# Attention and a token-mixing MLP on one core: late weights' loads tied to ScalarE's progress, the last two blocks turned into one tile and one product, and another order table

## The chip, the cores and the metric

The kernel runs on one core of a Trainium2 chip. The metric is the device time of one execution in microseconds (us); the kernel before has a median of 632.07 us over three runs (631.93 to 632.17). In the profile PE is TensorE's matmul side and PEld its weight loads, DVE is VectorE, ACT ScalarE, POOL GpSimd, SP the sync engine that issues most DMAs.

## The reference

With S = 2048 rows, D = 512 columns, H = 32 heads of 16 columns and F = 1376 hidden units:

```python
xn = layernorm(A_x)                           # per row, no scale or bias
# A: attention
q, k, v = split_heads(xn @ A_wqkv)            # 32 heads, 16 columns each
p = softmax(q @ k^T / 4)                      # 32 x 2048 x 2048
a = join_heads(p @ v) @ A_wo
# B: an MLP over the rows (tokens)
h = layernorm(xn)
u = gelu(h^T @ B_w1 + B_b1)                   # 512 x 1376
b = (u @ B_w2 + B_b2)^T
return A_x + a + b
```

`B_x` isn't used. Inputs and output are bfloat16.

## The kernel before

**Tiles and blocks.** The 2048 query rows are cut into four parts of 512 (`qb`), the 32 heads into eight groups of four. A part and a group make a block, 32 in all (`NBLK`), which are worked through one after the other. A block's four heads are four rows `r` of it, and the 2048 keys are 16 tiles `kt` of 128, so that a block has 64 score tiles of 128 keys x 512 queries, and the whole program 2048. `score_mm` (L758) makes one with K = 32 rows of TensorE's array (a head's 16 columns, the rest of QT being zero): four such products lie on the four row quarters of the array and can run beside each other. The result goes to one of eight PSUM banks of 512 f32.

**Two ways to exponentiate.** A score tile leaves PSUM by ACT or by DVE. `exp_tile` (L773) lets ACT exponentiate one, two or three banks at once into `pT`, or into slots in the memory of `wqkv_sb` once the weights there are used up. `first_planes` (L834) lets DVE make an integer approximation of the exponential, a "plane"; `make_plane` (L843) then derives two more planes from the first, by POOL (INT64_ADD) and in one place by DVE. Planes lie in `planes` and in the memory of `x_sb`, `xn_sb`, `xnT` and `w2blk`. `pv_mm` (L777) multiplies with V: one product for a tile from ACT, three for a tile from DVE, each on one of the four column quarters of the array and all into bank 7 (`PV_BANK`), where V's extra column of ones (`V17`) adds up the softmax's denominator in row 16 of each head's 32.

**Between blocks.** When a block's 64 tiles are through, `epi_steps` (L1063) copies bank 7 to SBUF, gathers the denominators by DMA (`den_scr`), inverts them (L1089), spreads them by two more DMAs (`rec_scr`, `denb`) and multiplies (L1105) into `oT`, which the output projection `op_mm` (L1026) reads. Two neighbouring blocks share a tile of 128 rows: the odd block's heads are moved into the gaps of the even one by the DMA `OT<-OT`. Block 30 has a shortened chain of its own without that move (`last`, `nr`), and block 31 is finished at the end by `tail_epilogue` (L1276), which turns bank 7 with DVE's transposes, so that the denominator lies beside its row, inverts, multiplies and turns back into `otmp`. As 30 and 31 lie in different tiles, the last 128 rows of A_wo are applied as two products, each with half of its rows zero: `wo_pad` and `op_half` (L1031).

**The rest of the work.** The projections to Q, K and V, both layer norms, the MLP (`ut_steps`, `yo_steps`) and the output projection are cut into chains of steps that are fitted between the scores. Most products of 128 columns are issued as four of 32 (`mm_full`, L651).

**The order.** What stands where on each engine is written out by hand in the string `ORDER`, which `replay` (L1180) reads: S are scores, E an exponential on ACT, F and L planes, P a group of four products with V, C the next step of a chain, H a quarter of such a step, U a product of the tail, Z zeros, G a copy of `part` into a bank. `Sched` (L306) records the operations, works out who must wait for whom from what they read and write, and puts the waits in. Every engine then runs its own list in order, and so does SP with its DMAs: a DMA that waits holds up all behind it on SP.

**The late weights.** `late_steps` (L949) is a chain that loads what the prologue doesn't need: b1, the first two column blocks of w1 (`w1_load`), `wo_c` (all of A_wo) and the eight strips of `wo_pad`. Its steps wait for nothing but the memory that they write.

Of the kernel before, what the change touches and what calls it, by code (L numbers as in the profile page):

```python
# [9 lines left out]
BF16 = mybir.dt.bfloat16  # L10
# [5 lines left out]
D = 512  # L16
# [42 lines left out]
NW1 = 2  # L59
# [14 lines left out]
C006C00C00S3000011025E20101E152S3032103114E22334E145C00Z7C1NC011C01C01C01C01C00C01C01C01C01C01C01C01C01C1OS3045056060  # L74
C1NE25667E108C01C01C01C0j3C1TC01C0jC0jS3074085096E2459AE16BC1UC022C01C1OC02P0000P333.S30A00B10C5C1OE201CDE15EC02C034
C1VC03C03C03P66.3C046C1WC04C04C04C04C04C03C04S10D2E12FC1PS30E00F10G4E20101E142C04P9.66C0jC04C055C1PC05S20H60I2C1PE163
E126P.999C05C061C04C1XS30J40K50L0E24578E109C06C1YC1iC06C1QC06C086PCCC.C1iC08C06C1iC1QS30M40N50O2E245ABE12CC1iC071C07
C07PFF.CC07C1iC08C090C1iC1RC1iS30P40Q50R6C1QE245DEE160C09C09C09C07C07C07C07Z7C09C0A2C0AC0AC07C0AC0AC0AC0AS10S0E101C1Z
S30T40U50V1E2452FE113C07C1aC0APIIFFC1RC0B6C0BC0AC0X0C0XC0BS30W40X50Y2H0XFC1RE24567E128C0XC0AC1bC0C6C0CC0CC0CPLLIIC1c
S10Z1H0XCE119C0CC1SS30a40d50b6E3456ABCPOOLLC0E2C0jC0EC1SS10e1H0XDE11DC0jC0D3C0DC0DC0DC0DC0DC0DC0DC0ES30f40h50i6H0XEC1S  # L80
C1fE3456012PRROOC0F1C0DC0FC0FC1dC0FC0G3C0GC0GC0DC0GC0GC0GC0FC0GC0GC0Y2C0jC1eC0YC0YC0GS10c1E11EC0XS10g3E133C0YC0GC1j
S30j40k50l6E3456678C1kC0H1C0YC0HS30m20n30o0E2239FE10AC1lC0HPUURRZ7C1mZ7C1nS30p40q50r6E2450CE16BC1oPXXUUC1pC0I1C0IC1q
C0IC0IC1rC0J3C0JC0JC0JC1sC0JC0JC0JC0JPaaXXC0IC0L2C0LC0LC0JC0LC0LS20s00t1E201DEC1tS30u40v50w3E24512E133C0JC0LC1uC0LC0L
C0LC1vC0LC0LC0LC0LC1wC0LC0LC0LPddaaC1xC0Z6C0LC0ZC0ZS30x00y10z2E20167E128C1yC0LS20-40_5E2459FC1gC1gC1gC1gC1gC1gC1gC1g
C1gC1gC1gC0ZPggddC1gC0M3C0MC0ZC0MC0MC0MC0MC0MC1gC0MC0MC0MC0MC0MC0MC0MC0MC0MC0a6C0aS313014112A0H0aDE2010AC0MC0aC0M
S316417515B0H0aCE245BCF12PjjggP..jjF13S31901A118A0H0aFE20112C1-C0N3C0NC0NC0NC0NC0NC0NC0NC0NF12S21B41C5H0aEE245DEC1-C0N
# [344 lines left out]
def bass_parallel_sum__softmax_full_mha__mixer_token_mlp__prompt_kernel(  # L431
# [18 lines left out]
    with ExitStack() as es:  # L450
# [142 lines left out]
        def ld_wo():  # L593
            return dma("sp", wo_c[:, :, :], A_wo.rearrange("(T q) n -> q T n", q=128), reads=[], writes=[("wo_c",)])
# [585 lines left out]
        def replay(text):  # L1180
# [5 lines left out]
            for k in it:  # L1186
# [76 lines left out]
                elif k == "U":  # L1263
                    c, T = divmod(num(), 5)
                    if T == 4 or (T == 0 and c > 1):
                        tail_bk[c] = num()
# [101 lines left out]
```

## Time and profile before

| | |
|---|---|
| median of three runs | 632.07 us |
| the profiled execution | 631.26 us |
| its span, first to last instruction | 629.5 us |
| PE, DVE, ACT, POOL busy | 98%, 92%, 98%, 68% |
| granted TensorE clock | 1.00 of full speed throughout |
| DMA | 30.02 MB, mean 48 GB/s |

The span is from the profiled execution; the time of the same execution is 1.8 us longer than its span, and the median is 0.8 us above it. In rows of groups the columns are: line, engine, operation, what is written and read, shapes, count, then busy time in us and mean ns of one, then idle time before and who ended it. In a timeline they are start and length in us, and a bracket holds the idle time of the engine just before. Busy time counts overlapping instructions of an engine once, so a mean length can be longer than the step from one to the next.

### The profile page before, as it was taken

The page shows a single profiled execution, that of the slowest core. Times are in us where ns is not written, and L with a number is a line of the kernel's source. Part 1 is how long each engine was busy: PE and PEld are TensorE (multiplying, and loading weights), DVE is VectorE, ACT ScalarE, POOL GpSimd, SP SyncE. Part 2 cuts the span into 40 slices and gives each one's busy share as a digit, 9 for nine tenths or more (in the row PEclk, how much of TensorE's full clock was granted, in tenths as well). Part 3 has the DMA queues.
Part 4 walks back from the last instruction along what each step waited for, and adds up shares of the span by engine and source line. Part 5 has one row for each costly group of instructions (what it writes and reads, how often), then busy time and mean ns, then how long its engine had stood idle before and what let it go on. Part 6 is the DMA issues. An engine that isn't in the chain of part 4 may idle for free.

```text
span 629.5 us, 20523 instructions
## 1 busy us (share of the span) xinstructions
PE 618.9 (98%) x8776; PEld 195.6 (31%) x8776; DVE 581.6 (92%) x889; ACT 616.3 (98%) x715; POOL 429.9 (68%) x625
## 2 busy tenths in 40 slices
PE   8989999999999999999999999999999999999997
PEld 4444342222232322222223323222322222232223
DVE  7989999989989999999999999998999899989996
ACT  7989999999999999999999999999999999999995
POOL 2105666866677777767688767867887678776775
PEclk9999999999999999999999999999999999999999
DMA  8050000112202122030121031112122121223001
GB/s 235 3 119 9 17 20 5 34 36 55 56 17 53 41 49 53 21 78 7 32 48 28 20 81 37 42 45 73 43 76 51 42 72 30 62 49 74 21 20 53
DMA packets 69957, 30.02 MB, mean 48 GB/s; under 512 B 56494, under 2 KB 66734, under 8 KB 69866
## 3 DMA queue, kind: packets, MB, share of 16 engines
q1 hardware_dynamic: 69434, 28.31, 18.5%
q8 instruction: 69, 1.13, 0.7%
q10 hardware_dynamic: 432, 0.39, 0.2%
q14 instruction: 22, 0.18, 0.1%
HBM read 22.15 MB, written 2.61 MB: 39 GB/s over the span
## 4 chain that ended last, share of the span: by engine, by line
PE 71%; ACT 25%; DVE 3%; issue 0%; POOL 0%; DVEq 0%; POOLq 0%
PE ps L786 27%; PE ps L761 24%; ACT pT L774 19%; PE ps L666 18%; ACT wqkv_sb L774 6%; DVE stats L603 0%; DVE KT L691 0%; DVE x_sb L838 0%; DVE xn_sb L838 0%; DVE xn_sb L629 0%; PE ps L678 0%; DVE planes L838 0%; PE ps L1142 0%; POOL jrow L523 0%; DVE V L691 0%
## 5 line engine op out<-in xcount | busy, mean ns | idle before, releaser
L774 ACT ACTIVATE pT<-ps 128x1024 bf16<-128x1024 f32 (+2 forms) x501 | 462.2, 1026 | 2.5 <-PE ps L659 1.5
L761 PE MATMUL ps<-QT,KT 32*128 32x512 bf16 x2048 | 254.0, 384 | 1.5 <-DVE KT L691 0.3
L838 DVE TENSOR_SCALAR planes<-ps 128x512 int16<-128x512 f32 (+1 forms) x255 | 188.7, 771 | 12.2 <-PE ps L659 6.6
L774 ACT ACTIVATE wqkv_sb<-ps 128x1024 bf16<-128x1024 f32 (+1 forms) x177 | 175.1, 1028 | 0.1
L786 PE MATMUL ps<-pT,V 128*32 128x512 bf16 x954 | 156.3, 386 | 0.0
L838 DVE TENSOR_SCALAR x_sb<-ps 128x512 int16<-128x512 f32 (+1 forms) x172 | 137.5, 825 | 13.8 <-PE ps L761 8.0
L761 PEld LDWEIGHTS ps<-QT,KT 32*128 32x128 bf16 x2048 | 67.3, 90 | 239.0 <-ACT pT L774 139.6
L786 PE MATMUL ps<-planes,V 128*32 128x512 bf16 x606 | 123.2, 384 | 0.0
L786 PE MATMUL ps<-x_sb,V 128*32 128x512 bf16 x496 | 102.2, 383 | 0.0
L848 POOL INT64_ADD planes<-planes x73 | 58.7, 807 | 50.0 <-DVE planes L838 46.3
L786 PE MATMUL ps<-wqkv_sb,V 128*32 128x512 bf16 x337 | 77.3, 386 | 0.0
L848 POOL INT64_ADD x_sb<-planes x81 | 63.1, 785 | 17.0 <-DVE planes L838 9.3
L838 DVE TENSOR_SCALAR xnT<-ps 128x512 int16<-128x512 f32 (+1 forms) x91 | 70.4, 801 | 4.6 <-PE ps L761 2.1
L786 PE MATMUL ps<-planes,V17b 128*32 128x512 bf16 x297 | 73.0, 384 | 0.0
L848 POOL INT64_ADD planes<-x_sb x73 | 57.6, 795 | 21.7 <-DVE x_sb L838 15.1
L838 DVE TENSOR_SCALAR xn_sb<-ps 128x512 int16<-128x512 f32 (+1 forms) x72 | 57.9, 826 | 3.2 <-PE ps L761 1.5
L786 PE MATMUL ps<-x_sb,V17b 128*32 128x512 bf16 x217 | 54.8, 384 | 0.2 <-DVE OT L1073 0.2
L666 PE MATMUL ps<-gT,w2blk 128*32 128x512 bf16 (+1 forms) x688 | 52.9, 383 | 0.0
L666 PE MATMUL ps<-xn_sb,w1blk 128*32 128x512 bf16 x624 | 49.6, 383 | 0.0
L786 PEld LDWEIGHTS ps<-pT,V 128*32 128x32 bf16 x954 | 39.0, 94 | 33.9 <-issue 29.6
L786 PE MATMUL ps<-xnT,V 128*32 128x512 bf16 x189 | 46.3, 384 | 0.0
L666 PE MATMUL ps<-xnT,wqkv_sb 128*32 128x512 bf16 (+3 forms) x612 | 40.6, 344 | 2.9 <-issue 1.3
(122 smaller groups left out, 890.5 us busy)
## 6 DMA issues: line engine op xcount, KB each, us to landing
w1blk<-in_B_w_dram SPq DMA_DIRECT2D x10, 512.0 KB
w2blk<-in_B_w_dram SPq DMA_DIRECT2D x16, 320.0 KB
denb<-rec_scr SPq DMA_DIRECT2D x16, 256.0 KB
xres<-in_A_x_dram SPq DMA_DIRECT2D x16, 128.0 KB, 3.3
QT<-qraw SPq DMA_DIRECT2D x120, 16.0 KB, 1.8
OT<-OT SPq DMA_DIRECT2D x60, 32.0 KB, 2.0
out_dram<-osb SPq DMA_DIRECT2D x14, 128.0 KB, 1.8
x_sb<-in_A_x_dram SPq DMA_DIRECT2D x2, 512.0 KB
```

What stands on the lines that cost most here:

```text
L666: op = sc.add("pe", lambda e, sl=sl, c=c: e.matmul(dst[sl, :], lhsT=lhsT[:, sl], rhs=rhs, start=start, stop=stop, tile_position=(0, 32 * c ...
L761: return sc.add("pe", lambda e: e.matmul(bank(bk), lhsT=KT[32 * r:32 * r + 32, T, 128 * kt:128 * (kt + 1)], rhs=QT[32 * r:32 * r + 32, slo ...
L774: return sc.add("act", lambda e: e.activation(slots(us), pick(ps3, bs), ACTF.Exp, scale=EXP_SCALE), reads=[("bank", b) for b in bs], write ...
L786: return sc.add("pe", lambda e: e.matmul(bank(PV_BANK)[32 * r:32 * r + 32, :], lhsT=vt_[:, off:off + 32], rhs=rhs, start=start, stop=stop, ...
L838: return sc.add("dve", lambda e: e.tensor_scalar(pick(plane_i[pb].rearrange("p (r n) -> p r n", n=512), ss), pick(ps3, bs), BIAS + SHIFT[0 ...
L848: return sc.add("pool", lambda e: e.int64_add(plane_q[pb][:, 0:128 * n], plane_q[pb0][:, 0:128 * n], -down * LANES), reads=rd, writes=wr, ...
```

## The change

It has three parts.

**Loads.** The two first loads of w1, the load of `wo_c` and the strips of the last weights are given one more dependence: the instruction that ACT was given last when the load was recorded (`extra=sc.streams["act"][-1:]`). SP issues such a load only when ACT is through with that instruction. In the order table the load steps now stand far apart.

**The end.** Block 30 takes the way of block 31: at its end `turned` turns bank 7 with two transposes into `ot`, `turned_rec` inverts 16 denominators per row, and `turned_mul` writes the result to columns 16 to 31 of each 32 of the tile `tb` (the memory of `zer`). Block 31 writes columns 0 to 15 of it. The tile is turned back once for both into `otmp`, and one product with `wo_s`, the last 128 rows of A_wo in the order that fits (strips of 16 swapped in pairs), takes the place of the two with `wo_pad`. Of the four strips of 128 output rows at the end (c = 0 to 3), ACT finishes the odd ones and DVE the even ones, in the order 0, 1, 2, 3; before, ACT finished 0 and 1, DVE 2 and 3, in the order 0, 2, 1, 3.

**The order.** The whole table is another one. It gives 1285 score tiles to ACT and 763 to DVE, where before it was 1291 and 757. ACT's exponentials of two tiles stay 601; those of one tile go from 71 to 47, those of three from 6 to 12. DVE's first planes of one tile go from 491 to 529, those of two tiles from 133 to 117. PE has 8778 instructions in both.

```diff
 ORDER = """
-C006C00C00S3000011025E20101E152S3032103114E22334E145C00Z7C1NC011C01C01C01C01C00C01C01C01C01C01C01C01C01C1OS3045056060
+C006C00C00S3000011022E3012012C00S3033104115E3345345Z7C00C1NC016C01C01S3040051062C1NE3012678C01C1TC01C01C01C01C01C01C0
...
-            return dma("sp", wo_c[:, :, :], A_wo.rearrange("(T q) n -> q T n", q=128), reads=[], writes=[("wo_c",)])
-
-        def ld_wop(e_, r):
+            return dma("sp", wo_c[:, :, :], A_wo.rearrange("(T q) n -> q T n", q=128), reads=[], writes=[("wo_c",)],
+                       extra=sc.streams["act"][-1:])
+
+        def ld_wos(e_, r):
+
             row = 3 * 128 + 32 * r + 16 * e_
-            return dma("sp", wo_pad[32 * r:32 * r + 16, e_, :], A_wo[row:row + 16, :], reads=[],
-                       writes=[("wo_pad", e_, r)])
+            p0 = 32 * r + 16 * (1 - e_)
+            return dma("sp", wo_s[p0:p0 + 16, :], A_wo[row:row + 16, :], reads=[], writes=[("wo_s", e_, r)],
+                       extra=sc.streams["act"][-1:])
...
-            z += [lambda bk, ft=ft: w1_load(ft) for ft in range(NW1)]
-            return z + [lambda bk: ld_wo()] + [lambda bk, e_=e_, r=r: ld_wop(e_, r) for e_ in range(2) for r in range(4)]
+            z += [lambda bk, ft=ft: w1_load(ft, sc.streams["act"][-1:]) for ft in range(NW1)]
+            return z + [lambda bk: ld_wo()] + [lambda bk, e_=e_, r=r: ld_wos(e_, r) for e_ in range(2) for r in range(4)]
...
-        def op_half(par, e_, sti, bk, first, last):
-            src = oT[:, par, 3, 128 * sti:128 * (sti + 1)] if e_ == 0 else otmp[:, 128 * sti:128 * (sti + 1)]
...
+        def op_last(sti, bk):
+            return mm_full(bank(bk), otmp[:, 128 * sti:128 * (sti + 1)], wo_s[:, :], 128, 512, False, True,
+                           [("otmp", sti)] + [("wo_s", e_, r) for e_ in range(2) for r in range(4)], bk)
...
+        def turned(dst, keys):
+
+            for h in range(2):
+                sc.add("dve", lambda e, h=h: e.transpose(dst[:, hs[h]], bank(PV_BANK)[:, hs[h]]),
+                       reads=[("bank", PV_BANK)], writes=[keys[h]])
+
+        def turned_rec(src3, c, rk, key, dk):
+            sc.add("dve", lambda e: e.reciprocal(den128[:, dk, c], src3[:, c, 16]), reads=[key], writes=[rk])
+
+        def turned_mul(src3, c, rk, key, dk, i0, zk):
+            n = c.stop - c.start
+            sc.add("dve", lambda e: e.tensor_tensor(tb3[:, c, i0:i0 + 16], src3[:, c, 0:16],
+                                                    den128[:, dk, c].unsqueeze(2).broadcast_to([128, n, 16]), ALU.mult),
+                   [key, rk], zk)
...
+            if b == NBLK - 2:
+
+                ot3 = ot.rearrange("p (c i) -> p c i", i=32)
+                c = slice(0, 16)
+                return [lambda bk: turned(ot, [ok, ok]), lambda bk: turned_rec(ot3, c, ("den", pi), ok, pi),
+                        lambda bk: turned_mul(ot3, c, ("den", pi), ok, pi, 16, [("zer",), ("zer2",)])]
...
-                dst, key = (osb[:, c, :], ("osb", c)) if c < 2 else (xres[:, c - 2, :], ("xres", c - 2))
-                if c < 2:
+                dst, key = (osb[:, c // 2, :], ("osb", c // 2)) if c % 2 else (xres[:, c // 2, :], ("xres", c // 2))
+                if c % 2:
                     copy("act", dst, bank(bk), [("bank", bk)], [key])
...
-            for c in (0, 2, 1, 3):
+            for c in range(4):
                 fin(c)
```

What moves on SP, early in the program: `QT<-qraw` spreads a block's queries, `den_scr`, `OT<-OT`, `den`, `rec_scr` and `denb` are the steps between blocks, `w1blk`, `wo_c` and `wo_pad` or `wo_s` the late loads. Before:

```order
L516 DMA b1r<-in_B_b_dram 1x96
L516 DMA w1blk<-in_B_w_dram 128x16x128 x2
L516 DMA wo_c<-in_A_wo_dram 128x4x512
L516 DMA wo_pad<-in_A_wo_dram 16x512 x8
L513 DMA den_scr<-OT 4x512
L516 DMA QT<-qraw 16x512 x8
```

Now, from the same place:

```order
L516 DMA b1r<-in_B_b_dram 1x96
L513 DMA den_scr<-OT 4x512
L516 DMA w1blk<-in_B_w_dram 128x16x128
L516 DMA QT<-qraw 16x512 x8
L516 DMA w1blk<-in_B_w_dram 128x16x128
L513 DMA den_scr<-OT 4x512
L516 DMA OT<-OT 16x512 x4
L513 DMA den<-den_scr 128x32
L513 DMA rec_scr<-den 128x32
L516 DMA wo_c<-in_A_wo_dram 128x4x512
L513 DMA denb<-rec_scr 128x1x512
```

The eleven late loads stood in one piece; now the first three lie on both sides of a block's queries and of its denominators' way, and the eight of `wo_s` follow one to three at a time over the next two blocks.

PE at the end of the program: `wo_c,oT` are products of the output projection with finished tiles, the others with V are the last block's. Before:

```order
L786 MATMUL ps<-planes,V 32x512
L786 MATMUL ps<-wqkv_sb,V 32x512 x4
L666 MATMUL ps<-wo_c,oT 32x512 x28
L666 MATMUL ps<-wo_pad,oT 32x512 x16
L666 MATMUL ps<-wo_pad,otmp 32x512 x16
```

Now:

```order
L667 MATMUL ps<-wo_c,oT 32x512 x8
L787 MATMUL ps<-pT,V 32x512 x2
L787 MATMUL ps<-wqkv_sb,V 32x512 x2
L667 MATMUL ps<-wo_c,oT 32x512 x40
L667 MATMUL ps<-wo_s,otmp 32x512 x16
```

The 16 products with `wo_pad,oT` are gone, and 40 instead of 28 products with `wo_c` stand behind the last group with V.

ACT's first exponentials, between the small steps of the layer norm (`mv`). Before:

```order
L774 ACTIVATE pT<-ps 128x1024
L774 ACTIVATE pT<-ps 128x512
L774 ACTIVATE pT<-ps 128x1024
L774 ACTIVATE pT<-ps 128x512
L610 ACTIVATE mv<-mv,epsb 128x2
```

Now:

```order
L775 ACTIVATE pT<-ps 128x1536 x2
L611 ACTIVATE mv<-mv,epsb 128x2
L614 ACTIVATE mv<-mv 128x2
L775 ACTIVATE pT<-ps 128x1536 x4
L611 ACTIVATE mv<-mv,epsb 128x2
```

Pairs and singles by turns have become triples there; six of the twelve triples stand in these rows.

493 lines of the change are left out of this document (238 added, 255 removed).

## The prediction

> **What bounds the kernel now.** I read the page first: busy shares (part 1), then the chain that ended last (part 4).
>
> ```profile
> span 629.5 us, 20523 instructions
> PE 618.9 (98%) x8776; PEld 195.6 (31%) x8776; DVE 581.6 (92%) x889; ACT 616.3 (98%) x715; POOL 429.9 (68%) x625
> PE 71%; ACT 25%; DVE 3%; issue 0%; POOL 0%; DVEq 0%; POOLq 0%
> ```
>
> Three engines are close to full, and the chain runs through PE and ACT by turns. A busy PE is not PE at its peak, so the next question is which of the two is really full. The chain in order of time has a long piece on ACT alone, and pieces on PE that are whole groups of four products:
>
> ```profile
> 53.44 0.76 PE ps L786 x12
> ...
> 111.99 25.32 ACT pT L774 x28
> ...
> 249.31 0.98 PE ps L786 x16
> ```
>
> 28 exponentials of two tiles follow each other at 25.32 / 28 = 0.904 us without a gap: there ACT cannot go faster. On PE four more products cost 0.98 - 0.76 = 0.22 us, so a group of four products, one to each quarter of the array, has a step of 0.22 us. The instruction groups with shapes kept apart give ACT's sizes (last columns: busy us, mean ns of one):
>
> ```profile
> L774 ACT ACTIVATE pT<-ps 128x1024 bf16<-128x1024 f32 x443 | 429.8, 1069 | 2.2 <-PE ps L659 1.5
> L774 ACT ACTIVATE wqkv_sb<-ps 128x1024 bf16<-128x1024 f32 x158 | 163.5, 1071 | 0.0
> L774 ACT ACTIVATE pT<-ps 128x512 bf16<-128x512 f32 x53 | 32.0, 619 | 0.3
> L774 ACT ACTIVATE wqkv_sb<-ps 128x512 bf16<-128x512 f32 x18 | 11.1, 624 | 0.1
> L774 ACT ACTIVATE pT<-ps 128x1536 bf16<-128x1536 f32 x5 | 7.3, 1468 | 0.0
> L774 ACT ACTIVATE wqkv_sb<-ps 128x1536 bf16<-128x1536 f32 x1 | 1.5, 1486 | 0.0
> ```
>
> A pair lasts 1.069 us but steps at 0.904, so consecutive ones overlap by 0.165 us; with the same overlap a single tile steps at about 0.454 us and three tiles at 1.303 us (estimates from these rows). ACT's exponentials then need 601 x 0.904 + 71 x 0.454 + 6 x 1.303 = 583 us. ACT is the engine with the least slack, PE is close behind it, and DVE follows.
>
> The windows by stage show that the middle has no hole, and one hole early:
>
> ```profile
> 44.00:46.00 2.00, 0.71 (x8) 0.11 (x6) 0.99 (x2) 0.93 (x2) 0.00 (x0) 1.00 0.84 244
> 280.00:320.00 40.00, 39.75 (x514) 11.63 (x512) 38.61 (x55) 40.00 (x46) 30.21 (x31) 1.00 0.12 27
> ```
>
> (Columns: PE, PEld, DVE, ACT, POOL busy, then clock, DMA share, GB/s.) At 44 to 46 us PE, DVE and ACT all stand still; at 280 to 320 us ACT is busy for all 40 us.
>
> **Term 1, the late loads.** The timeline around the hole, SP's queue first:
>
> ```profile
> 38.01 1.67 SPq L516 DMA_DIRECT2D w1blk<-in_B_w_dram  x2
> 39.72 2.11 SPq L516 DMA_DIRECT2D wo_c<-in_A_wo_dram  x1
> 41.88 4.91 SPq L516 DMA_DIRECT2D wo_pad<-in_A_wo_dram  x8
> 45.50 0.61 PE L666 MATMUL ps<-xnT,wqkv_sb 128*32 128x512 bf16 x6 [1.29 <-issue]
> 46.47 1.94 ACT L774 ACTIVATE pT<-ps 128x1024 bf16<-128x1024 f32 x2 [1.54 <-PE ps L659]
> ```
>
> PE waited 1.29 us for nothing that the profile shows ("issue"), and ACT 1.54 us for PE. No queue of data explains it, but the instruction queue does:
>
> ```profile
> w1blk<-in_B_w_dram SPq DMA_DIRECT2D x1, 512.0 KB
> q8 instruction: 69, 1.13, 0.7%
> 35.20:42.70 7.50, 7.24 (x183) 3.89 (x183) 7.25 (x25) 7.50 (x11) 0.00 (x0) 1.00 0.61 119
> q8 instruction: 1, 0.02, 5.5%
> 132.50:138.50 6.00, 6.00 (x84) 1.56 (x83) 5.81 (x9) 6.00 (x8) 3.90 (x6) 1.00 0.43 90
> q8 instruction: 1, 0.02, 1.3%
> ```
>
> The second row is the whole run: 69 instruction transfers against 2 x 8776 PE records, one for every 254. The third row holds 183 + 183 = 366 PE records, and the DMA view of that window lists no instruction transfer at all; the next one is in 42.7 to 44.2 us (fourth row), in the middle of the weights' loads. So PE's next instructions came late behind two loads of w1 (512 KB each, first row) and those of wo, and PE ran dry. The last two rows are a check from later: in 132.5 to 138.5 us one load of w1 and one instruction transfer share the DMA engines, and PE is busy for 6.00 of 6.00 us.
>
> After the change nothing of this stands at 38 us: by the steps of ACT's exponentials ahead of each wait, the first w1 load is let go at about 53 us, the second some 15 us later, wo_c another 17 us later, and the strips of wo_s come one or three at a time after 100 us. That is the case of the check row. The first product with w1 stands about 70 us of exponentials behind the first load, so nothing waits for the later arrival. Bounds: 0, if PE is late at that place for another reason, and 1.54 us, ACT's whole wait; I take **-1.4 us**, near the row. SP now waits for ACT eleven times, with QT's spreads and the denominators' transfers queued behind it. The nearest row is SP's own wait in that chain:
>
> ```profile
> SPq L513 <- DVE den L1089: 66.1, 13, 9.3
> ```
>
> SP stands there 5 us on the average and 9.3 at the longest (total us, times, longest), and the chain that ended last has no DMA in it, so I take 0 and keep +1 us, for one late multiplication, as a bound.
>
> The page "Runtime: NRT & Kernel Launch" of the Trainium skill (section "Instruction fetch mechanics") says that an engine streams its program in 16 KiB blocks through a queue of its own, that a crossing is mostly hidden, and that PE's store holds 2048 instructions. The 16 KB blocks agree with the trace; by the rest PE could not have run dry here, and this term would be 0. The 366 records without a block, and the standstill behind them, speak against it; the case has its own chance below.
>
> **Term 2, the end.** The timeline after the last product with V:
>
> ```profile
> 622.19 0.39 PE L786 MATMUL ps<-wqkv_sb,V 128*32 128x512 bf16 x4
> 622.40 1.68 PE L666 MATMUL ps<-wo_c,oT 128*32 128x512 bf16 x28
> 622.63 0.78 DVE L1285 STREAM_TRANSPOSE denb<-ps 128x256 f32<-128x256 f32 x2 [0.28 <-PE ps L786]
> 623.91 1.04 PE L666 MATMUL ps<-wo_pad,oT 128*32 128x512 bf16 x16
> 623.94 0.76 DVE L1295 STREAM_TRANSPOSE otmp<-zer 128x256 bf16<-128x256 bf16 x2
> 624.78 1.04 PE L666 MATMUL ps<-wo_pad,otmp 128*32 128x512 bf16 x16
> 625.22 1.09 ACT L690 ACTIVATE osb<-ps 128x512 bf16<-128x512 f32 x2 [3.19 <-PE ps L666]
> 625.65 1.29 DVE L1307 TENSOR_TENSOR xres<-ps,w1blk 128x512 bf16<-128x512 f32 x2 [0.95 <-PE ps L666]
> ```
>
> PE has 28 + 16 = 44 products to do here while DVE turns the last block; the products with otmp start twelve steps behind the last PV group, (624.78 - 622.19) / 12 = 0.216 us each. The first half of DVE's last transpose ends at 623.94 + 0.38 = 624.32, so PE is the later of the two by about 0.2 us. After the change 40 products stand there: one step less, -0.2 us, and DVE's chain is then about level with PE. The finishing order changes too. Now ACT takes strips 0 and 1, DVE strips 2 and 3, and DVE ends last at 625.65 + 1.29 = 626.94. With DVE on strips 0 and 2 and ACT on 1 and 3, DVE can start when strip 0 is there (about 625.0) and ends at about 626.3, ACT from 625.2 with 0.55 each at about 626.3: another -0.4 us. Together **-0.6 us**; bounds 0 (DVE's chain is what PE waits for) and -0.9. Block 30's DMAs and its multiplication vanish from the end at no gain: DVE idled 0.28 us for PE ahead of L1285, so nothing before that on DVE held it up.
>
> **Term 3, who takes the tiles.** Counted over both orders, the exponentials change from 601 pairs, 71 singles and 6 triples to 601, 47 and 12. ACT saves 24 x 0.454 - 6 x 1.303 = 3.1 us; six tiles less go through it. DVE gets these six: its one-tile planes rise from 491 to 529, its two-tile planes fall from 133 to 117.
>
> ```profile
> L838 DVE TENSOR_SCALAR planes<-ps 128x512 int16<-128x512 f32 x213 | 140.4, 682 | 10.8 <-PE ps L659 6.6 <-PE ps L761 3.2
> L838 DVE TENSOR_SCALAR planes<-ps 128x1024 int16<-128x1024 f32 x42 | 51.3, 1222 | 1.4 <-PE ps L761 1.1
> ```
>
> By busy time 140.4 / 213 = 0.66 and 51.3 / 42 = 1.22 us: DVE does 38 x 0.66 - 16 x 1.22 = 5.6 us more, out of 629.5 - 581.6 = 48 us idle. At the handover from block 30 to 31 two transposes (0.78 us at L1285) stand for one pass over a tile (0.68 us in the row above): **+0.1 us** on the path, once. POOL's additions rise by a few microseconds of its 200 idle ones. PE has the same 8778 products (12 more with V, 16 fewer at the end, 4 more with zeros), five steps fewer when grouped, but it changes 14 times more often between scores and the other products. What a change costs:
>
> ```profile
> 616.84 0.39 PE L761 MATMUL ps<-QT,KT 32*128 32x512 bf16 x3
> 617.16 0.39 PE L786 MATMUL ps<-pT,V 128*32 128x512 bf16 x1
> ```
>
> 617.16 - 616.84 = 0.32 us against a step of 0.22, so 14 x 0.10 - 5 x 0.22 = **+0.3 us** on PE. How much of ACT's 3.1 us reaches the end depends on PE keeping up: bounds 0 and -3.1. ACT is the fuller one (40.00 of 40 us), yet the chain is 71% PE, so I take two thirds, **-2.1 us**, and +0.2 us for DVE's share, whose work is hidden by its 48 idle us; if that cover is gone, up to +5.6 us.
>
> **Sum.** -1.4 - 0.6 + 0.1 - 2.1 + 0.3 + 0.2 = -3.5 us. The profiled execution took 631.26 us (span 629.5), and would go to 627.8; the runs shown have a median of 632.07, so I forecast **628.6 us**. About 0.2%, 1.3 us, is what a measurement can tell from no change. The whole order is new, and how its waits fall by chance I cannot read from before: ACT is busy for 616.3 us while its exponentials at their closest need 583; the 33 us between are its other work and overlap lost where one waits for its scores, and the latter may shrink or grow. I allow 2 us either way.
>
> **The rivals.**
> PE sets the pace. If ACT's saving is eaten by PE's alternation, terms 1 and 2 remain: -1.4 - 0.6 + 0.1 + 0.3 = -1.6, 630.5 us. For it: the chain's 71%. Against: 40.00 of 40 us on ACT.
> The standstill is not the loads' doing, or comes back at the next load: term 1 is 0, 630.0 us. Against: the check row. By the Trainium skill's page named above it would be this one. Together with the first rival nothing measurable is left, 631.9 us.
> Slower: DVE becomes the bound. At 280 to 320 us it is busy for 38.61 of 40 us, and 5.6 us more spread evenly makes 38.97. It decides when DVE reads a bank so late that PE's next scores wait for it. Today these waits are small beside those for ACT:
>
> ```profile
> PEld ps L761 <- ACT pT L774: 139.6, 361, 0.5
> PEld ps L761 <- DVE planes L838: 6.2, 18, 0.4
> ```
>
> If half of the 5.6 us lands and ACT's saving is lost, -1.6 + 2.8 = +1.2, 633.3 us; all of it, 636.1.
>
> **Chances.** Forecast 0.50 (its own range 626.5 to 630.5), PE's pace 0.18, loads no cause 0.10, both 0.07, DVE 0.15. Faster: 0.47 of the first, about half of the second and most of the third, 0.64; slower 0.15; the rest, 0.21, within 0.2%. The range 625.5 to 633.2 takes term 3 whole, the larger ends of terms 1 and 2 and a little of ACT's waits below, and about half of the DVE case above.
>
> **What would show it.** Right: no PE wait for "issue" over 1 us between 40 and 90 us, an instruction transfer about every 254 PE records there, ACT's exponentials busy about 3 us less with windows still at 40.00 of 40, and DVE's last addition over 4.1 us after the last PV group begins instead of 4.75. Wrong: the same ACT time with more PE in the chain (first rival), a standstill at 54 or 69 us (second), or PE's waits for DVE planes several times 6.2 us (third).

## The result, and the profile after

| | before | after |
|---|---|---|
| median | 632.00 us (6 runs, 631.56 to 632.34) | 628.58 us (6 runs, 628.49 to 628.74) |
| profiled execution | 631.26 us | 628.49 us |
| its span | 629.5 us | 626.7 us |

The ratio is 0.9946, with a 95% interval of [0.9933, 0.9959]: faster by 3.4 us, against 3.5 forecast from the profiled execution and a forecast of 628.6 us. One execution of a later kernel, the profiled one of `a_flood300`, took 1700 us at a granted clock of 0.32, and neither its time nor its trace is used. That a sum comes out right doesn't say that its terms do, so what follows takes the terms one by one. The page of the kernel after, span, busy times and chain:

```profile
span 626.7 us, 20538 instructions
PE 617.2 (98%) x8776; PEld 195.4 (31%) x8776; DVE 584.9 (93%) x911; ACT 613.6 (98%) x697; POOL 431.1 (69%) x623
PE 82%; ACT 10%; DVE 7%; DMA 0%; issue 0%
```

ACT has 616.3 - 613.6 = 2.7 us less to do (about 3 was forecast), DVE 3.3 us more (5.6 was forecast), PE 1.7 us less. The chain has moved from 71% PE and 25% ACT to 82% and 10%; what that is worth is tested below. The windows of the kernel after at the places shown of before, with the instruction transfers of the first one, and the waits for DVE named in the third rival:

```profile
35.20:42.70 7.50, 7.15 (x180) 3.70 (x181) 7.50 (x26) 6.99 (x12) 0.00 (x0) 1.00 0.06 14
q8 instruction: 2, 0.03, 2.4%
44.00:46.00 2.00, 2.00 (x67) 1.08 (x53) 1.24 (x3) 2.00 (x4) 0.00 (x0) 1.00 0.03 8
280.00:320.00 40.00, 39.54 (x513) 11.78 (x505) 38.97 (x56) 39.93 (x45) 30.69 (x39) 1.00 0.20 44
PEld ps L762 <- DVE planes L839: 6.2, 18, 0.4
```

The hole at 44 to 46 us is closed: PE and ACT are busy for 2.00 of 2 us there, and the DMA engines for 3% of the time instead of 84%. Between 35.2 and 42.7 us, where before 366 PE records passed without an instruction transfer, two of them now arrive for 361 records. These counts depend on where the window begins. If the window of the DMA view is made narrow, before has a transfer at 35.10 us, just ahead of it, and the next at 42.75; after has them at 35.50, 41.60 and 45.50. From one to the next that is 7.65 us and 379 PE records before, and 6.1 us and 312 records after. The windows from such a transfer on, in before up to the standstill, in after up to the next transfer:

```profile
35.15:44.20 9.05, 8.79 (x254) 4.98 (x253) 8.15 (x27) 9.05 (x13) 0.00 (x0) 1.00 0.71 138
35.55:41.60 6.05, 5.76 (x157) 3.11 (x155) 6.05 (x21) 5.80 (x10) 0.00 (x0) 1.00 0.05 10
```

So in before PE didn't stand still when the 366 records were through. It went on for 1.45 us behind the start of the late transfer, stopped after 254 + 253 = 507 records, two times the average of 254 between transfers, and went on at 45.50 us, 2.75 us behind that start.

DVE at 280 to 320 us is at 38.97 us, to the hundredth what the third rival had assumed. That is chance, as over the whole run DVE got 3.3 us more and not 5.6. PE's scores wait for DVE's planes no longer than before (6.2 us, 18 times), and with the rows of the other tiles that DVE's first planes go to (`x_sb`, `xnT`, `xn_sb`, `w2blk`) it is 15.6 us before and 16.3 now. By these waits DVE did not become the bound; `a_dve` below asks again.

**A new hole.** Where block 30 hands over to 31, the timeline of after has one that before doesn't have:

```profile
605.06 1.04 POOL L849 INT64_ADD x_sb<-x_sb  x1 [0.95 <-DVE x_sb L839]
605.15 1.22 DVE L1078 TENSOR_TENSOR zer<-OT,den 128x256 bf16<-128x256 f32 x1
606.30 1.21 DVE L839 TENSOR_SCALAR xn_sb<-ps 128x1024 int16<-128x1024 f32 x1
607.57 0.39 PE L762 MATMUL ps<-QT,KT 32*128 32x512 bf16 x2 [0.42 <-DVE xn_sb L839]
608.00 1.23 DVE L839 TENSOR_SCALAR planes<-ps 128x1024 int16<-128x1024 f32 x1 [0.49 <-PE ps L762]
609.29 3.85 ACT L775 ACTIVATE pT<-ps 128x1024 bf16<-128x1024 f32 x4 [0.82 <-PE ps L762]
```

Read it from the bottom: ACT stands for 0.82 us because PE's scores are late, PE's scores are late because DVE freed their bank late (`<-DVE xn_sb`), and DVE was late because of a multiplication of block 30 (L1078) that lasts 1.22 us. It ends at 606.37, 0.27 us after POOL's addition ended (605.06 + 1.04 = 606.10).

**The end.** The timeline of after from the last product with V on, and then the last two output transfers of before:

```profile
619.67 0.40 PE L787 MATMUL ps<-pT,V 128*32 128x512 bf16 x2
619.88 2.35 PE L667 MATMUL ps<-wo_c,oT 128*32 128x512 bf16 x40
621.54 0.77 DVE L1303 STREAM_TRANSPOSE otmp<-zer 128x256 bf16<-128x256 bf16 x2
622.03 0.14 PEld L667 LDWEIGHTS ps<-wo_s,otmp 128*32 128x32 bf16 x8 [0.29 <-DVE otmp L1303]
622.04 1.05 PE L667 MATMUL ps<-wo_s,otmp 128*32 128x512 bf16 x16
622.50 1.29 DVE L1315 TENSOR_TENSOR xres<-ps,w1blk 128x512 bf16<-128x512 f32 x2 [0.19 <-PE ps L667]
622.71 1.08 ACT L691 ACTIVATE osb<-ps 128x512 bf16<-128x512 f32 x2 [3.15 <-PE ps L667]
623.22 0.34 SPq L516 DMA_DIRECT2D out_dram<-xres  x1
623.60 0.43 SPq L516 DMA_DIRECT2D out_dram<-osb  x1
623.83 0.35 ACTq L516 DMA_DIRECT2D out_dram<-osb  x1
624.07 0.45 SPq L516 DMA_DIRECT2D out_dram<-xres  x1
```

```profile
626.75 0.46 SPq L516 DMA_DIRECT2D out_dram<-osb  x1
626.97 0.35 ACTq L516 DMA_DIRECT2D out_dram<-xres  x1
```

The products with `otmp` start 622.04 - 619.67 = 2.37 us after the last PV group, where it was 624.78 - 622.19 = 2.59: the saved step of PE, 0.22 us, is there. Their weight loads waited 0.29 us for DVE's transposed tile, the products themselves show no wait, so PE and DVE are about level here, as forecast. DVE's last addition ends at 623.79, 4.12 us after that group instead of 4.75, as forecast. But from the group to the end of the span it is 7.03 us instead of 7.31: only 0.28 us of the 0.63 arrived. The issues show where the rest went. In both kernels SP issues three of the four transfers, one behind the other, and ACT the one of strip 3. In before strip 3 is also DVE's last addition: it ends at 626.94, its issue starts at 626.97 and is through at 627.32. In after DVE's last addition is strip 2. Its issue stands on SP behind that of strip 1 (623.60 + 0.43 = 624.03), starts at 624.07, 0.28 us behind the addition's end, and is through at 624.07 + 0.45 = 624.52. From the last issue's end to the span's end it is 2.18 us in both.

### The profile page after: what moved, and what is told of

It reads as the page before. It is cut to its first block, busy times and chain, and to the rows that moved or that the text cites. A ratio compares the mean times of both kernels' runs of the same rounds, so it can differ in the third digit from the quotient of the medians.

```text
span 626.7 us, 20538 instructions
## 1 busy us (share of the span) xinstructions
PE 617.2 (98%) x8776; PEld 195.4 (31%) x8776; DVE 584.9 (93%) x911; ACT 613.6 (98%) x697; POOL 431.1 (69%) x623
## 3 DMA queue, kind: packets, MB, share of 16 engines
HBM read 21.88 MB, written 2.59 MB: 39 GB/s over the span
## 4 chain that ended last, share of the span: by engine, by line
PE 82%; ACT 10%; DVE 7%; DMA 0%; issue 0%
PE ps L787 33%; PE ps L762 29%; PE ps L667 20%; ACT pT L775 7%; ACT wqkv_sb L775 3%; DVE x_sb L839 1%; DVE planes L839 1%; DVE stats L604 1%; DVE xn_sb L839 1%; DVE xn_sb L630 1%; DVE xnT L692 1%; DMA x_sb<-in_A_x_dram 0%; DVE xnT L839 0%; DVE KT L692 0%; DVE V L692 0%
## 5 line engine op out<-in xcount | busy, mean ns | idle before, releaser
L839 DVE TENSOR_SCALAR planes<-ps 128x512 int16<-128x512 f32 (+1 forms) x268 | 200.4, 777 | 14.6 <-PE ps L660 6.9
L775 ACT ACTIVATE wqkv_sb<-ps 128x1024 bf16<-128x1024 f32 (+2 forms) x172 | 174.7, 1038 | 0.1
L787 PE MATMUL ps<-planes,V 128*32 128x512 bf16 x574 | 116.1, 384 | 0.0
L787 PE MATMUL ps<-x_sb,V 128*32 128x512 bf16 x477 | 98.1, 383 | 0.0
L787 PE MATMUL ps<-wqkv_sb,V 128*32 128x512 bf16 x335 | 83.3, 386 | 0.0
L787 PE MATMUL ps<-planes,V17b 128*32 128x512 bf16 x314 | 77.4, 384 | 0.1
L849 POOL INT64_ADD x_sb<-planes x64 | 53.0, 832 | 20.3 <-DVE planes L839 17.6
L787 PE MATMUL ps<-xnT,V 128*32 128x512 bf16 x204 | 49.0, 383 | 0.0
L787 PE MATMUL ps<-xn_sb,V 128*32 128x512 bf16 x203 | 43.8, 383 | 0.0
```

Of the source, the lines that this page charges most:

```text
L775: return sc.add("act", lambda e: e.activation(slots(us), pick(ps3, bs), ACTF.Exp, scale=EXP_SCALE), reads=[("bank", b) for b in bs], write ...
L787: return sc.add("pe", lambda e: e.matmul(bank(PV_BANK)[32 * r:32 * r + 32, :], lhsT=vt_[:, off:off + 32], rhs=rhs, start=start, stop=stop, ...
L839: return sc.add("dve", lambda e: e.tensor_scalar(pick(plane_i[pb].rearrange("p (r n) -> p r n", n=512), ss), pick(ps3, bs), BIAS + SHIFT[0 ...
L849: return sc.add("pool", lambda e: e.int64_add(plane_q[pb][:, 0:128 * n], plane_q[pb0][:, 0:128 * n], -down * LANES), reads=rd, writes=wr, ...
```

## The experiments

The theory at this point: the lump of late loads starved PE of instructions; ACT's saved work carries the new order; the handover gives some of it back. Rivals: the loads are no cause; PE sets the pace and not ACT; DVE pays for ACT's gain. The kernel before was run beside each group of experiments. Its medians there were 631.82 (12 runs), 631.84 (25), 632.11 (17) and 631.77 us (8), with single runs from 630.8 to 633.9 us (the last section says what the upper ones have in common), so that differences against it carry an uncertainty of about 1 us. Runs of kernels that keep the new order and the spaced loads lie within 0.4 us of each other, and differences between them are good to about 0.2 us.

### The loads: put back in one lump, and spaced in the old order

`a_flood` is the kernel after with all eleven loads behind b1's, without waits (the two `extra=` of `wo_c` and `wo_s` go too):

```diff
...
-            z += [lambda bk, ft=ft: w1_load(ft, sc.streams["act"][-1:]) for ft in range(NW1)]
-            return z + [lambda bk: ld_wo()] + [lambda bk, e_=e_, r=r: ld_wos(e_, r) for e_ in range(2) for r in range(4)]
+            def rest(bk):
+                ld_b1(1)
+                for ft in range(NW1):
+                    w1_load(ft)
+                ld_wo()
+                for e_ in range(2):
+                    for r in range(4):
+                        ld_wos(e_, r)
+            return [lambda bk: ld_b1(0), rest] + [lambda bk: None] * (NW1 + 9)
```

> The changed kernel, but with all eleven late loads in one piece behind b1's and without the waits for ScalarE, as the kernel before has them; its order table and its end stay. Theory (the loads hold up TensorE's next instructions): 1.2 to 1.6 us slower than the changed kernel, 629.8 to 630.2 us, with a wait of PE for issue of over 1 us and a hole of about 1.5 us on ACT between 43 and 47 us, and one instruction transfer there that comes after clearly more than 254 PE records. Rival (the standstill came from the old order): within 0.3 us of the changed kernel, 628.3 to 628.9 us.

Measured: 629.85 us (629.10 to 630.33), 1.3 us more than after, as the theory had it. In its profiled run, the fastest of the five, the hole is back at the old place, in the windows and in the timeline. The second row is the window from an instruction transfer (35.60 us) up to the standstill:

```profile
44.00:46.00 2.00, 1.55 (x56) 0.90 (x49) 0.85 (x2) 2.00 (x4) 0.00 (x0) 1.00 1.03 286
35.60:45.45 9.85, 9.54 (x249) 5.03 (x247) 9.05 (x28) 9.62 (x15) 0.00 (x0) 1.00 0.74 154
45.87 0.34 PE L665 MATMUL ps<-wqkv_sb,xnT 128*32 128x128 bf16 x9 [0.45 <-issue]
47.22 1.94 ACT L773 ACTIVATE pT<-ps 128x1024 bf16<-128x1024 f32 x2 [0.46 <-PE ps L760]
```

PE waits for "issue" again while the DMA engines are full (share 1.03), and ACT waits for PE behind it. The hole is smaller than expected: 0.45 us on PE and 0.46 on ACT instead of over 1 and 1.5, and this run took only 0.61 us more than the profiled one of after (629.10 and 628.49). The next transfer comes late again, at 43.35 us, after 366 records; PE stands still after 249 + 247 = 496 records and goes on at 45.87, 2.5 us behind the start of that transfer. The runs scatter over 1.2 us.

`b_spaced` is the counterpart: the kernel before, whose eleven loads are let go behind chosen exponentials.

```diff
-            z += [lambda bk, ft=ft: w1_load(ft) for ft in range(NW1)]
-            return z + [lambda bk: ld_wo()] + [lambda bk, e_=e_, r=r: ld_wop(e_, r) for e_ in range(2) for r in range(4)]
+            return z + [lambda bk: None] * (NW1 + 9)
...
+        LATE = {49: lambda: w1_load(0, last_act()), 66: lambda: w1_load(1, last_act()), 84: lambda: ld_wo(last_act())}
+        for i_, n_ in enumerate((102, 104, 106, 109, 120, 123, 126, 129)):
+            LATE[n_] = lambda e_=i_ // 4, r=i_ % 4: ld_wop(e_, r, last_act())
```

> The kernel before, its order table and its end untouched, but the late loads issued one by one at the places in ScalarE's work where the changed kernel has them (about 53, 69, 86 us, then the eight strips from 100 us on), each waiting for ScalarE's last instruction. Theory: 1.2 to 1.6 us faster than the kernel before, 630.4 to 630.8 us, without the hole at 44 to 46 us. Rival (the loads are no cause): within 0.3 us of 632.0 us.

Measured: 629.73 us (629.63 to 631.62, 7 runs), ratio 0.9968 [0.9957, 0.998], 2.1 us less than before, more than the 1.2 to 1.6 expected. The window of its hole:

```profile
44.00:46.00 2.00, 2.00 (x46) 0.60 (x32) 1.67 (x4) 2.00 (x4) 0.00 (x0) 1.00 0.03 8
```

So the loads are the cause in both orders, and the second rival falls. Between the two profiled runs the gain is 631.26 - 629.80 = 1.46 us, the size of the hole there (1.54); between the medians it is larger.

### Which part of it: the waits, or the places?

`a_nowait` keeps the table's places for the loads and takes the added dependences on ACT away (`extra=sc.streams["act"][-1:]` in three places).

> The changed kernel without the added waits for ScalarE; the load steps stay apart in SP's queue. Theory: SP reaches the first load of w1 behind the first block's denominators, at about 46 us, and the loads after it come with the other DMAs; the dense part of TensorE's work is nearly over there, so 0 to 0.5 us slower than the changed kernel (628.6 to 629.1 us). Rival (only the waits keep the loads apart): 1.2 us slower or more, 629.8 us.

Measured: 628.53 us (628.42 to 628.69), as after. The order table does the spacing; the eleven waits that SP got are worth nothing, and cost nothing.

`a_flood300` adds to the kernel after, at ACT's 300th exponential, three loads of 512 KB from one place in DRAM to another, each a column block of w1 in rows of 256 bytes. They add work and change no value.

```diff
...
+                    if n_e[0] == 300:
+                        for f in range(3):
+                            dma("sp", flood[f], B_w1[:, 128 * f:128 * f + 128], reads=[], writes=[("flood", f)],
+                                extra=sc.streams["act"][-1:])
```

> The changed kernel with three more loads of 512 KB in one piece, from w1 to a scratch in HBM in rows of 256 bytes, issued at ScalarE's 300th exponential (about 290 us); nothing reads them. Theory (what counts is whether the next 254 records' worth of TensorE instructions lasts longer than the loads, 10 us here against 5 at 40 us): no change, within 0.3 us of 628.6 us, PE busy throughout. Rival (any such burst slows the engines): 1 to 1.5 us slower, 629.6 to 630.1 us.

Measured: 628.6 us (four runs, 628.40 to 628.68), as after. A lump at that place does no harm, then. How fast PE goes through its instructions at the two places is worked out from the window rows of after: 361 records in 7.50 us at 35 us are, at 254 to a transfer, one transfer in 5.3 us; 513 + 505 records in 40 us at 280 us are one in 10 us. That fits the theory, but doesn't show that the pace makes the difference: these loads also end in DRAM and not in SBUF, and no usable trace of them was kept.

### Who sets the pace?

The same question was put to each engine: add work to it, evenly over the run, and see how much of it the time grows by. All of these add work and change no value.

`a_act` and `b_act` add 12 passes of 128x512 on ACT, one at every 40th exponential:

```diff
...
+                    if n_e[0] in range(110, 590, 40):
+                        sc.add("act", lambda e: e.activation(scr[:, :], zer[:, 0:512], ACTF.Identity), [("zer",)], [("scr",)])
```

> The changed kernel with 12 more ACT passes over one tile (128x512 bf16 from constant zeros to a scratch that nothing reads), one after every 40th exponential from the 110th on: about 12 x 0.5 = 6 us of ACT work, no other engine has more. If ACT sets the pace (the forecast, two thirds of ACT's saving reach the end): 4 to 6 us slower than the changed kernel, 632.6 to 634.6 us. If PE sets it (the chain after is 82% PE, 10% ACT): 0.6 to 2 us slower, 629.2 to 630.6 us.

> The kernel before with the same 12 more ACT passes, about 6 us. If ACT sets the pace there: 4 to 6 us slower than the kernel before, 636 to 638 us. If an added microsecond on ACT counts as its share of the chain (25%): 1 to 2 us slower, 633 to 634 us.

`a_pe` and `b_pe` add 28 groups of four products with zero weights to the PV bank:

```diff
...
+                    if n_e[0] >= 110 + 16 * n_e[1] and n_e[1] < 28:
...
+                            zero_rows(PV_BANK, rows, [r for r in rows if (pv[0], r) not in n_done], False)
```

> The changed kernel with 28 more groups of four products with zero weights, added to the bank of the block that is open (they change no sum), about every 16th exponential from the 110th on: 28 x 0.216 = 6 us of PE work. If PE sets the pace: 4.5 to 6.5 us slower than the changed kernel, 633.1 to 635.1 us. If ACT sets it and PE has slack: 0 to 2 us slower, 628.6 to 630.6 us.

> The kernel before with the same 28 groups of four zero-weight products on PE (6.05 us of steps) as were put into the kernel after; it adds work and changes no value. Theory (three engines work interlocked and each added microsecond is paid nearly in full, before as well as after): 4.8 to 6.0 us more than before, 636.8 to 638.0 us. Rival (ScalarE alone set the pace of the kernel before and PE had slack there, as the 40.00 of 40 us busy time of ScalarE suggests, so that the new order gained by taking work off ScalarE alone): 0 to 2.5 us more, 632.0 to 634.5 us.

`a_dve` adds ten multiplications of 128x512 f32 on DVE:

```diff
...
+                    if n_e[0] in range(110, 590, 48):
+                        sc.add("dve", lambda e: e.tensor_tensor(scr[:, :], scr[:, :], scr[:, :], ALU.mult), [("scr",)], [("scr",)])
```

> The changed kernel with 10 more DVE passes (128x512 f32, scratch times scratch), one after every 48th exponential from the 110th on: about 10 x 0.6 = 6 us of DVE work, near the 5.6 us that the change moved to DVE. If DVE has become the bound (the rival on the slower side): 4 to 6 us slower, 632.6 to 634.6 us. If its work is hidden: 0 to 1.5 us slower, 628.6 to 630.1 us.

What one addition costs its engine is read from the timeline where it stands, ACT's in `a_act` and PE's in `a_pe`:

```profile
146.32 0.63 ACT L1240 ACTIVATE scr<-zer 128x512 bf16<-128x512 bf16 x1
146.84 1.03 ACT L776 ACTIVATE pT<-ps 128x1024 bf16<-128x1024 f32 x1
```

```profile
123.30 0.40 PE L1161 MATMUL ps<-zer 128*32 128x512 bf16 x4
123.52 0.38 PE L787 MATMUL ps<-pT,V 128*32 128x512 bf16 x2
```

The next instruction starts 0.52 us after ACT's pass and 0.22 us after PE's group, so 12 x 0.52 = 6.2 us and 28 x 0.216 = 6.05 us were added. DVE's ten took 8.8 us by the group's row, 8.0 us counted by the steps to the next instruction. Those that no addition of POOL holds up step at 0.60 us, so that about 2 of the 8.0 us are waits for POOL (last section) and not work of DVE:

```profile
L1242 DVE TENSOR_TENSOR scr<-scr 128x512 f32<-128x512 f32 x10 | 8.8, 882 | 0.0
```

| kernel | added | median | more than its base | paid |
|---|---|---|---|---|
| `a_act` | 6.2 us on ACT | 634.35 us (634.17 to 634.47) | 5.8 us | 93% |
| `a_pe` | 6.05 us on PE | 633.84 us (633.68 to 634.03) | 5.3 us | 87% |
| `a_dve` | 8.0 us on DVE | 633.74 us (633.57 to 633.87) | 5.2 us | 65% |
| `b_act` | 6.2 us on ACT | 638.36 us (4 runs, 637.22 to 639.60) | 5.7 us at the same clock | 91% |
| `b_pe` | 6.05 us on PE | 636.51 us (635.94 to 638.17) | 4.4 us | 73% |

Two of the four runs of `b_act` had a granted clock of 0.997, so it is compared at the same clock: its other two average 637.48 us against a median of 631.81 for before, these two 639.29 against 633.63. The difference of all medians would be 6.5 us, more than was added.

No engine has the slack that its idle time suggests. That holds for DVE too: the 5.2 us of `a_dve` lie in the range expected for DVE as the bound. The rival of `b_pe`, at most 2.5 us, falls, and so does the idea that one engine alone sets the pace, before or after; its own expectation of 4.8 us or more was missed by 0.4, within the scatter of the kernel before. Now the chain that ended last, in this order for `a_act`, `a_pe` and `a_dve`:

```profile
ACT 54%; PE 41%; DVE 4%; DMA 0%; issue 0%
```

```profile
PE 83%; ACT 11%; DVE 5%; DMA 0%; issue 0%
```

```profile
PE 81%; DVE 13%; ACT 5%; issue 1%; POOL 0%; DVEq 0%; POOLq 0%
```

Twelve passes, 1% of ACT's work, turn its share from 10% to 54%. Where engines run neck and neck the chain tells which was last at each place, not by how much. That after's share of PE was 82% did not mean that ACT's work had become free.

### The handover

`a_latemul` takes the reciprocal and the multiplication of block 30 out of their place at the handover and puts them behind block 31's last tile, into DVE's idle time before the end. The edit is in the order table, two steps of chain 2:

```diff
-...E2454CC1MC1MC2SS4VO...E223KOC2SL57...PheaPXdgdU92...
+...E2454CC1MC1MS4VO...E223KOL57...PheaPXdgdC2SC2SU92...
```

> The kernel after with block 30's last two VectorE steps (the reciprocal's strip and the multiplication of its turned output, 1.22 us in the trace of after at 605.15, of which most is a wait for GpSimd) taken out of their place at the handover from block 30 to 31 and put behind block 31's last tile, into VectorE's idle time ahead of the last additions. Theory (the step of 1.22 us on VectorE is what leaves ScalarE without scores for 0.82 us at 609.3): the hole there goes, 0.5 to 0.8 us off the time of after, 627.8 to 628.1 us. Rival (the hole is PE's, from the products of the new order around block 30's end): as after, 628.6 us within 0.2.

Measured: 627.94 us (627.78 to 628.14), ratio to before 0.9932 [0.9915, 0.9949], 0.64 us less than after, as the theory had it. Its timeline at the place of the hole:

```profile
605.31 1.22 DVE L837 TENSOR_SCALAR xn_sb<-ps 128x1024 int16<-128x1024 f32 x1 [0.49 <-PE ps L760]
608.35 3.85 ACT L773 ACTIVATE pT<-ps 128x1024 bf16<-128x1024 f32 x4
```

DVE's pass starts a microsecond sooner (605.31 instead of 606.30), and the same four exponentials start 0.94 us sooner, with no wait. The hole was DVE's, and this version is faster than both kernels.

### The end

`a_tail16` adds 16 products with zero weights between those with `wo_c` and those with `otmp`, to see whether PE or DVE is the later one there:

```diff
             for c in range(4):
+                zero_rows(tail_bk[c], range(4), (), False)
```

> The kernel after with 16 more products with zero weights (one group of four to each of the four last PSUM banks) between the 40 products with wo_c and those with the last block's turned output; it adds work and changes no value. Theory (at the end PE is the later one, at 0.216 us for a group of four, so that the step saved in the change is worth its length): 0.6 to 0.86 us more than after, 629.2 to 629.45 us. Rival (VectorE's transposes of the last block are what the last products wait for, and the saved step was worth nothing): within 0.2 us of after, 628.6 us.

Measured: 630.54 us (12 runs, 630.40 to 630.77), 2.0 us more than after, outside both expectations. The timeline says why:

```profile
621.90 1.04 PE L1161 MATMUL ps<-zer 128*32 128x512 bf16 x16
622.99 0.49 DVE L1078 TENSOR_TENSOR zer<-denb,den 128x128 bf16<-128x128 f32 x2 [1.90 <-PE ps L1161]
623.90 1.05 PE L667 MATMUL ps<-wo_s,otmp 128*32 128x512 bf16 x16 [0.96 <-DVE otmp L1305]
```

The added products read `zer` as their moving side, and DVE's multiplication overwrites `zer`: it had to wait 1.90 us for them. The experiment made its own wait and settles nothing. What stays is the trace of after alone, where the step saved is seen in PE's start (2.37 us instead of 2.59).

`a_fin` is the kernel after with the finishing order of before:

```diff
-                if c % 2:
+                if c < 2:
                     copy("act", dst, bank(bk), [("bank", bk)], [key])
...
-            for c in range(4):
+            for c in (0, 2, 1, 3):
                 fin(c)
```

and in the table the zeros and copies go to strips 0 and 1 (`U42`, `G02`, `U94`, `G14`), with the products in matching order.

> The kernel after with the finishing order of before: ScalarE takes strips 0 and 1, VectorE strips 2 and 3, and the four additions, passes and output transfers stand in the order 0, 2, 1, 3; the products with wo_c change places to match, 40 in number as in after. The prediction's step (the new finishing order ends VectorE 0.4 us sooner, and the kernel with it): 629.0 us, 0.3 to 0.5 more than after. The rival from the trace of after (SyncE issues three of the four output transfers one behind the other, 0.34 to 0.45 us each, so that the last issue, not VectorE's last addition, sets the end): 628.5 to 628.75 us, as after.

Measured: 628.63 us (628.51 to 628.70), as after. Its timeline:

```profile
619.80 0.38 PE L787 MATMUL ps<-pT,V 128*32 128x512 bf16 x2
623.04 1.29 DVE L1315 TENSOR_TENSOR xres<-ps,w1blk 128x512 bf16<-128x512 f32 x2 [0.62 <-PE ps L667]
624.37 0.35 ACTq L516 DMA_DIRECT2D out_dram<-xres  x1
```

DVE ends 4.53 us after the last PV group, 0.41 later than in after, just what the prediction had said; but the last issue is through 4.92 us after it, against 624.52 - 619.67 = 4.85. The finishing order is worth under 0.1 us: with the old one DVE ends later (624.33), but its last transfer goes out at once on ACT's queue (624.37); with the new one DVE ends sooner, and the transfer waits for SP.

## Why the prediction was right

The sum was right, and so were the signs. The end and the handover came out 0.3 and 0.5 us worse than forecast, and the loads and the order made up for it; that the total was met within 0.1 us is luck.

| term | forecast | measured |
|---|---|---|
| late loads | -1.4 | -2.1 in the old order, -1.3 in the new |
| the end | -0.6 | -0.28 |
| handover from block 30 to 31 | +0.1 | +0.6 |
| the new order as a whole | -1.6 | -1.6 to -2.3, as what is left |

The row of the handover is what `a_latemul` won back, so it is the reciprocal and the multiplication without the two transposes. The last row is a remainder, not a measurement of its own: from `b_spaced` to `a_nowait` it is -1.2 us, from before to `a_flood` -2.0; less the end (-0.28) and the handover (+0.64) that gives -1.6 and -2.3. Why the loads cost more in the old order than in the new is open. The scatter is as large as the difference, and a trace shows one run of each; if runs at a granted clock of 0.997 or less are left out on both sides, the -2.1 becomes -2.0.

**The late loads.** Cause and size held: without the lump PE has no wait for "issue" between 40 and 90 us, and with it there is one in both orders. That PE lacks instructions there is inferred from the late transfers, no row says it. The prediction's "366 records without a block, and the standstill behind them" read the row too narrowly: the window begins just behind a transfer and ends at the start of the next, and PE stood still only after 507 records, when the late transfer had begun 1.45 us before. The forecast took the row of the one hole, -1.4; what the kernel loses varies from run to run, and the runs of `a_flood` scatter by 1.2 us against 0.3 for `a_nowait` beside it. The Trainium skill, page "Runtime: NRT & Kernel Launch", section "Instruction fetch mechanics", calls a crossing mostly hidden. The time of `a_flood300` agrees with it, and `a_flood` and `b_spaced` are cases where it wasn't hidden; by the page this term would have been 0. The bound of +1 us for SP's waits was not needed: `a_nowait` is no faster.

**The end.** The step of PE was right (0.22 us). The failing step was "DVE ends last [...] another -0.4 us": DVE's end moved as said, but the kernel doesn't end with DVE. It ends with the last issue of an output transfer, and the new order puts the one that belongs to DVE's last addition on SP, behind another one: 0.25 us more of waiting and 0.10 us more of issuing than on ACT's queue, of the 0.63 that DVE gained. The rows for it were in the trace of before: the last issue was ACT's, through at 627.32, 0.38 us after DVE's end at 626.94.

**The handover.** The failing step was "two transposes (0.78 us at L1285) stand for one pass over a tile". It counted what stands on DVE where the bank is read, and left out the reciprocal and the multiplication that follow in the same stretch; the multiplication alone took 1.22 us. In before block 30's multiplication stood at the end (621.67 us), ahead of a wait of DVE, and the prediction itself had noted that it leaves there "at no gain". A moved step has to be priced at the place that it goes to.

**The new order.** ACT's busy time came about as counted (-2.7 us against 3.1), DVE's did not (+3.3 against 5.6), and the waits for DVE stayed about what they were. What was wrong is the reason given for DVE's share, "hidden by its 48 idle us". `a_dve` shows that added work there is paid at 65%. And "two thirds of ACT's saving" was a guess from the chain's share; a microsecond added to ACT was paid at 93%. At these prices ACT's 2.7 us and DVE's 3.3 us would nearly cancel (-2.5 + 2.1 = -0.4 us, an estimate from these rows), and the remainder is four to six times that. So no run shows what the gain of the new order is made of; that its additional planes cost little because the whole order was laid out with them is possible and not shown. The remainder of -1.6 to -2.3 also holds what the new order loses at its beginning. The windows of before and of after:

```profile
20.00:40.00 20.00, 18.77 (x413) 9.62 (x410) 19.35 (x56) 19.52 (x35) 2.76 (x7) 1.00 0.08 19
```

```profile
20.00:40.00 20.00, 17.79 (x388) 9.39 (x384) 19.01 (x56) 18.79 (x33) 1.87 (x6) 1.00 0.04 10
```

ACT is busy for 18.79 us there instead of 19.52, and PE for 17.79 instead of 18.77: the new table's start is less dense than the old one's. No run took this piece alone.

**The rivals.** PE's pace: the chain went its way (82% PE), the time did not, and `a_act` shows ACT still to be paid for. The loads as no cause: refuted both ways. DVE as the bound: the time went the other way and the waits did not grow, but `a_dve` shows that further work on DVE is paid too, so what was refuted is the loss and not the price.

## What to carry to other kernels

A hole that no data transfer explains, with PE waiting for "issue", is worth a look at the instruction queue: loads that nothing needs yet should be spread out, or put where, as in `a_flood300`, PE goes slowly through its instructions. Where three engines are at 92 to 98%, neither idle time nor shares of the chain are slack; add a known amount of work to one engine and see what is paid. At the end of a kernel, follow the work to the last issue of an output transfer and to the queue that it stands on, and count every step that a move brings to its new place.

## What the runs showed of the hardware that was not expected

A multiplication on DVE with both inputs in SBUF stands still until a running addition of POOL is through. The one at the handover took 1.22 us and ended 0.27 us after POOL's; the added ones of `a_dve` took 680 ns at the least and 1399 ns at the most, and those of 0.95, 1.10, 1.25 and 1.40 us each ended 0.53 or 0.54 us after the addition that POOL had begun before them. It holds the other way round too: where the multiplication had begun first (197.50 us), POOL's addition beside it took 1.40 us and the one before it 1.04. The multiplication into `oT`, by line, in the trace of after:

```profile
L1124 DVE TENSOR_TENSOR oT<-OT,denb x15: 681/682/1232, 98.5 to 609.1; 128x512 bf16<-128x512 f32 x15
```

(Duration in ns: least, median, greatest.) The Trainium skill, page "SBUF — State Buffer", section "SBUF: two separate sides", says that such an operation and a GpSimd operation that reads SBUF exclude each other for a whole instruction, and the traces agree.

How far PE's store of instructions reaches is seen only indirectly. With full DMA queues PE stood still 507 records (before) and 496 records (`a_flood`) behind the start of the transfer before the late one, about two times the usual 254, and went on 2.75 and 2.5 us behind the start of the late one. In after that transfer starts at 41.60 us, about 3.6 us ahead of the 507th record, and nothing stands still.

The kernel before has two groups of times. Of its 62 runs beside the experiments 15 had a mean granted clock of 0.996 or 0.997 and took 632.9 to 633.9 us; the other 47, at 0.999 or 1.00, took 630.8 to 632.3. `b_spaced`, `b_act` and `b_pe`, which keep the old order, show the lower clock in 5 of 17 runs; the kernels with the new order never fall below 0.998 in their 73 runs, `a_flood` among them. So it goes with the old order or the old end and not with the lump of loads. No profiled run had the lower clock, so where in the program it drops, and why, is open.
